# Converting weights beside pairs two and three: loads a whole tile ahead, three pieces per tile, 16 and 24 tiles

## The chip, the core and the metric

The kernel runs on one core of a Trainium2 chip. The metric is the time of one execution on the device in microseconds (us), lower is better; times of several executions are given as their median. The engines are PE (TensorE, matrix products), DVE (VectorE), ACT (ScalarE), POOL (GpSimd) and SP (SyncE, which here only issues DMAs).

## What is computed

The reference chains three parts, all on float inputs:

```python
attn = softmax(scale * q_c @ k_c.T)      # chunks of 64 rows, 8 batches x 8 heads x 576 rows
x = (attn @ v_c)                         # reshaped to 4608 x 512
x = ((x @ w_a) * (x @ w_b)) @ w_out      # first gated product, d_ff = 1536
h = ((x @ w1) * (x @ w2)) @ w3           # second gated product, d_ff = 1024
out = h @ w_out2
```

The weights of the first product are `w_a`, `w_b`, `w_out`; those of the second are `w1`, `w2`, `w3` and its own `w_out`.

## The kernel before

**Tiles and pairs.** The 4608 rows are nine blocks of 512. Eight of them go as four pairs, numbered by `sb` from 0 to 3; the last block stands alone. The program runs the first gated product over all pairs and the lone block, then the second one over them again. "Pair one, two, three" below are `sb` = 1, 2, 3 of the first product; pair zero is done by a plain scheme at the start, the others with seven products of half-size blocks (Strassen's scheme) instead of eight.

**A step.** `strassen_step` (line 873) does one block of 128 columns of the hidden width. There are 12 such steps in a pair. A step emits seven products `P5, P1, P2, P6, P3, P7, P4`, each of six matmuls (line 807), ACT copies three of them out of PSUM (line 892), DVE adds three (lines 895) and multiplies the last (line 922). PSUM banks are used again within the step, so a product waits for the eviction of an earlier one. Between them stand four parts of the output product of the step before (`Second.part`, line 836, three matmuls each). 42 + 12 = 54 matmuls of 512 columns make a step.

**Work beside the steps.** Seven times in a step `point` is called. It lets a `Track` (line 51) emit further pieces of work: each piece has a cost in estimated microseconds, and a point emits pieces until the cost done has reached its share of the total. In a pair these pieces are the attention of the next pair (`attention_pieces`, line 990: eight units beside pair two, four beside pair three) and, beside pairs two and three alone, the conversion of later weights (`later_conv`, line 1102). `merged` (line 1111) interleaves the two lists by the middle of each piece's cost. Since every engine runs its instructions in the order of emission, the place of a piece fixes what stands behind it on DVE, ACT, POOL and SP.

**The conversion.** 40 tiles of the second product's weights are converted beside pairs two and three. The weights lie in memory as 64-bit numbers, and `Conv` (line 160) makes 32-bit ones of a tile of 128 x 512. `load` (line 167, DMA on SP's queue, line 173) brings 512 KB into one of three buffers (`slot(3)`). `s1` (line 177) is one DVE operation (L179) and one of ACT (L180); `s2` (line 182) is three of DVE (L185, L188, L189) and an addition on POOL (L195). The result is stored with a DMA on ACT's queue (L157), which is put off: `store` (line 135) with wait 5 is issued after five ticks, one tick per product or part, or at the next `tick(True)`.

**The pump.** `Pump` (line 197) holds the tiles in order. `run` (line 219) issues the stores that wait, then calls `begin(self.done + 2)`, which runs `s1` of the next tile if it is loaded, then `s2` of the current one. In `later_conv` a tile has two pieces, `run` with cost 2.2 and `load` with cost 0.6. `load` asks for the tile after the next, so the load of tile i + 2 is emitted after run of tile i, and its `s1` in run of tile i + 1. The buffer of tile i + 2 is that of tile i - 1, so SP's load waits until the store of tile i - 1 has landed. Fourteen tiles stand beside pair two, the other 26 beside pair three (line 1325).

**SP's queue.** SP issues, in order of emission, the weight parts of the step after the next (`load_part`, line 710, L713 and L715, each waiting until PE has freed its buffer), the output weights (L701), the attention's loads (L148) and the conversion's loads (L173).

Of the kernel before, what the change touches and what calls it, by code (L numbers as in the profile page):

```python
# [78 lines left out]
def chunk_attention_two_gated_products(  # L79
# [30 lines left out]
    NF = [FA // P, FB // P]  # L110
# [40 lines left out]
    def tick(every=False, loads=0):  # L151
        settle(asks["done"] + loads)
        for s in stores:
            s[0] += 1
        while stores and (every or stores[0][0] > 1):
            _, to, src = stores.popleft()
            nc.scalar.dma_start(to, src)  # L157


    class Conv:  # L160
# [3 lines left out]
        def __init__(self, src, name, k=1):  # L164
            self.src, self.k, self.nm = src, k, name
# [31 lines left out]
    class Pump:  # L197
# [3 lines left out]

        def __init__(self):
            self.jobs, self.done, self.begun, self.loaded = [], 0, 0, 0
            self.cap, self.last = 0, None

        def add(self, jobs):
            self.jobs.extend(jobs)
# [11 lines left out]
        def run(self):  # L219
            assert self.done < self.loaded  # L220
            tick(True)
            last, self.last = self.last, None
            if last:
                last[0]()
            self.begin(self.done + 2)
            c, sink, eng = self.jobs[self.done]
            c.s2(eng)
            if last:
                last[1]()
            self.last = sink(c.w)  # L230
            self.done += 1
# [371 lines left out]
    def lone_pieces(x32, nm):  # L603

        xq = [pool.tile([P, 2, 2, NT], F32R, tag=f"xo{5 + K}", name=f"xl{K}{nm}") for K in range(2)]

        def one(kt):
            to = xq[kt // 2][:, kt % 2]
            split(to[:, 0], to[:, 1], x32[kt], nc.vector)

        return xq, [(0.7, False, lambda kt=kt: one(kt)) for kt in range(KM)]
# [98 lines left out]
    def load_part(ph, f, i):  # L710
        t = w_tile(4 * (f % 2) + i, f"w{ph}_{f}_{i}")
        if i < 3:
            nc.sync.dma_start(whole(t).bitcast(F32), dw[ph][f][0 if i == 0 else i + 1])  # L713
        else:
            nc.sync.dma_start(  # L715
                t[:, 0].rearrange("p s k n -> p (s k n)").bitcast(F32), dw[ph][f][1][:, NT:]
            )
        pairs.setdefault((ph, f), {})[i] = t
# [287 lines left out]
    def attention_begins(units):  # L1006
        for u in units[:2]:
            u.load1()
            u.load2()
# [11 lines left out]
    def o2_pieces():  # L1021
        got = deque()

        def load(i):
            if i < NF[1]:
                got.append(load_small(do2[i], f"o2_{i}"))

        def one(i):
            if i % 2 == 0:
                tag = ["Y0", "Y1", "Y2", "xo0"][i // 2]  # L1030
                wo2.append(pool.tile([P, 2, 2, DM], F32R, tag=tag, name=f"wo2_{i // 2}"))
            t = wo2[i // 2][:, i % 2]
            split(t[:, 0], t[:, 1], got.popleft(), nc.vector)
            load(i + 3)

        for i in range(3):
            load(i)
        return [(0.7, False, lambda i=i: one(i)) for i in range(NF[1])]

    def load_w3(n):  # L1040
        if n < 2 * NF[1]:
            w3f.append(load_small(dw3[n // 2][n % 2], f"w3_{n}"))
# [28 lines left out]
    with tc.manual_schedule():  # L1071
# [3 lines left out]
        pump = Pump()  # L1075
# [13 lines left out]
        def slot(kind):  # L1089
            slots["n"] += 1  # L1090
            n = slots["n"]
            return dict(tag=["Y0", "Y1", "Y2", "xo4", "xo5", "xo6"][n % kind])

        def conv_piece():
            def emit():
                pump.run()
                while pump.loaded < min(pump.cap, pump.done + 3):
                    pump.load(slot(6))

            return (2.9, False, emit)  # L1100

        def later_conv(n):


            def load():
                if pump.loaded < pump.done + 2:
                    pump.load(slot(3))

            return [p for _ in range(n) for p in ((2.2, False, pump.run), (0.6, False, load))]

        def merged(*lists):

# [8 lines left out]
        def unit_list(sb):  # L1121
            js = [LONE] if sb == NSB else [2 * sb, 2 * sb + 1]
            cls = TurnedOnPE if sb == 1 else Unit
            return [cls(j, hp, T) for T, j in enumerate(js) for hp in range(NHP)]
# [48 lines left out]
        for n, (T, f) in enumerate(order):  # L1173
            if T == 0:
                conv = Track([conv_piece()] * (1 if f == 0 else 3), 5 if f + 1 < AHEAD else 8)
                if f + 1 == NF[0]:
                    conv = None
# [5 lines left out]
            def point(pe=True):  # L1183
                if conv:
                    conv.point(pe)
                (at or late).point(pe)
# [18 lines left out]
        def summed(ph, f, n):  # L1205
            tag = dict(tag=f"Y{n % 3}")
            return Sums(ph, f, tag)
# [87 lines left out]
        for ph, sb in [(0, sb) for sb in range(1, NSB + 1)] + [(1, sb) for sb in range(NSB + 1)]:  # L1295
            lone = ph == 0 and sb == NSB
            begins = ph == 1 and sb == 0
            if begins:
                state["outs"] = Outs(1, 2 * NSB + 1)
            state["outs"].ahead(2)  # L1300
            if lone:
                x, pieces = lone_pieces(x32, f"{ph}{sb}")
                pieces = pieces + o2_pieces()
            elif not begins:
                x, pieces = strassen_pieces(x32, f"{ph}{sb}", sb == NSB)
            if ph == 0 and sb == 1:
                for f in range(2):
                    first_sums[f] = summed(ph, f, f)
                    first_sums[f].load()
                for f in range(2):  # L1310
                    for i in (0, 3):
                        load_part(ph, f, i)
                pieces = pieces + first_sums[0].pieces()
            steps, at, conv = NF[ph], [], []
            if ph == 0 and not lone:
                units = unit_list(sb + 1)
                attention_begins(units)
                work = attention_pieces(units)
                n_pts = PTS * steps + steps - 4
                if sb == 2:  # L1320
                    pump.cap = len(pump.jobs)
                    pump.load(slot(3))
                    pump.load(slot(3))
                if sb >= 2:
                    conv = later_conv(14 if sb == 2 else pump.cap - 14 - 3 * NF[0])
                    work = merged(work, conv)
                    n_pts = PTS * steps
                at.append(Track(work, n_pts - 3))
            if not begins:
                burst(ph, j + 1, places, pieces, [] if conv else at, state.pop("ready", None))  # L1330
            if lone:
                got = []
                for n_ in range(4):
                    load_w3(n_)
                at.append(Track(between(got), 5 * steps - 15))
                xs = {}

                def next_x():
                    diffs = deque()
                    for i in range(2):  # L1340
                        t = pool.tile([P, 4, NT], F32, tag=f"G{i}", name=f"xd{i}")
                        diffs.extend(t[:, n_] for n_ in range(4))
                    xs["x"], xs["pieces"] = strassen_pieces(got, "10", diffs=diffs)

                early = [(0.1, False, lambda: (at[0].finish(), next_x()))]
                early += [(0.7, False, lambda n_=n_: xs["pieces"][n_][2]()) for n_ in range(18)]
                late = Track(early, 11)
                class After:
                    n = 0

                    def point(self, pe=True):
                        self.n += 1
                        if self.n > 5 * steps - 15:
                            late.point(pe)

                    def finish(self):
                        late.finish()

                at.append(After())
                lone_steps(ph, x, at)  # L1360
                for p in xs["pieces"][18:]:
                    p[2]()
                x32, x = got, xs["x"]
                continue
            if ph == 1 and sb < NSB:
                got = []
                js = [LONE] if sb == NSB - 1 else [2 * sb + 2, 2 * sb + 3]
                at.append(Track(x2_pieces(js, got), PTS * steps - 3))
            j, places = block_steps(ph, sb, x, at)
            if ph == 0:  # L1370
                x32 = [u.x32 for u in units]
            elif sb < NSB:
                x32 = got
# [47 lines left out]
```

## Time and profile before

| what | value |
|---|---|
| median of 3 runs | 1804.84 us (1803.17 to 1807.74) |
| the profiled execution's own time | 1824.92 us |
| its span, first to last instruction | 1823.1 us |
| mean granted clock of TensorE | 0.948 of 2.4 GHz |
| busy: PE, DVE, ACT, POOL | 1625.3, 888.3, 552.9, 449.7 us |
| moved by DMA | 409.55 MB, mean 225 GB/s |

The profiled execution is a single one and took 20.1 us more than the median. Times inside it are told from the start of its span. Busy time of an engine is the time in which it executes, waits not counted. The granted clock is the share of full speed that the chip's throttle gave to TensorE, at one of two levels at any moment, 1.2 or 2.4 GHz. L12 is line 12 of the kernel; SPq and DVEq are an engine's queue. "A <- B" in a wait means that A waited for B; in an instruction "out<-in" are the tiles that it writes and reads. The tiles of the conversion are `cv_o`, `cv_w` and `cv`, by the weight that they come from.

### The profile page before, as it was taken

Reading aid. Unit: us, or ns where it says so; the run is one execution under the profiler, and the core shown is the slowest. Engines: PE = TensorE matmul, PEld = TensorE weight load, DVE = VectorE, ACT = ScalarE, POOL = GpSimd, SP = SyncE. Lnnn points to the kernel's source line nnn. Section 1 sums busy time; section 2 is a strip of 40 time slices with the busy share of each in tenths; the row PEclk is TensorE's granted clock in tenths of the full one; section 3 lists DMA queues with packets and bytes.
Section 4 is the critical chain, followed back from the end, with each engine's and each line's share of the span. In section 5 each row is a group of like instructions: output and inputs, shape, how many; then the busy total and the mean of one; then the engine's idle time right before and its main releaser. Section 6 shows DMA issues by size and latency. Waiting matters only on the chain.

```text
span 1823.1 us, 24483 instructions
## 1 busy us (share of the span) xinstructions
PE 1625.3 (89%) x8968; PEld 1289.9 (71%) x8968; DVE 888.3 (49%) x1460; ACT 552.9 (30%) x989; POOL 449.7 (25%) x350
## 2 busy tenths in 40 slices
PE   5789999889998887897887797999999999999998
PEld 3567777667776665675665676778877877878887
DVE  5658756565763554564455533345234252252231
ACT  4434434222242221242221242223132142242232
POOL 1223323111141221242232240001232231231232
PEclk8789999999999998998898898999999999999999
DMA  8658766776778677586775577878666666676685
GB/s 209 219 172 262 254 202 173 226 215 188 246 223 238 194 199 205 193 249 221 231 228 191 194 256 265 325 296 300 208 225 225 208 222 228 208 231 208 196 280 176
DMA packets 302071, 409.55 MB, mean 225 GB/s; under 512 B 176000, under 2 KB 196480, under 8 KB 301952
## 3 DMA queue, kind: packets, MB, share of 16 engines
q1 hardware_dynamic: 265568, 318.85, 57.9%
q10 hardware_dynamic: 36384, 89.14, 12.8%
q8 instruction: 71, 1.16, 0.3%
q14 instruction: 48, 0.39, 0.1%
HBM read 321.91 MB, written 85.98 MB: 224 GB/s over the span
## 4 chain that ended last, share of the span: by engine, by line
PE 40%; DMA 5%; DVE 2%; issue 2%; POOL 1%; ACT 1%; SPq 0%; ACTq 0%; POOLq 0%; DVEq 0%
PE P L807 22%; PE acc L836 12%; PE wf L1060 3%; DMA cv<-in_moe_w_dram 2%; PE pa0L L793 2%; PE pb0L L793 2%; DMA d<-cv 1%; DMA wo<-dwo 1%; DMA w<-dw 0%; DVE c L895 0%; PE w3p L1050 0%; ACT ev L845 0%; DMA su<-d 0%; DMA x2d<-ev 0%; POOL gl_5b L243 0%
## 5 line engine op out<-in xcount | busy, mean ns | idle before, releaser
L807 PE MATMUL P<-xP,w 128*128 128x512 f32 (+1 forms) x3192 | 777.0, 397 | 102.1 <-DVE c L895 51.2
L807 PEld LDWEIGHTS P<-xP,w 128*128 128x128 f32 x3192 | 597.2, 196 | 249.9 <-DVE c L895 60.8
L895 DVE TENSOR_TENSOR c<-P,c 128x512 f32<-128x512 f32 (+1 forms) x228 | 149.7, 660 | 341.4 <-PE P L807 332.6
L892 ACT COPY c<-P 128x512 f32<-128x512 f32 (+1 forms) x228 | 128.1, 564 | 229.2 <-PE P L807 219.8
L923 POOL TENSOR_TENSOR G<-c,c 128x512 f32<-128x512 f32 x68 | 88.5, 1302 | 416.5 <-DVE c L895 416.2
L242 ACT CAST gh<-c 128x512 fp32r<-128x512 f32 x68 | 42.2, 621 | 356.0 <-DVE c L922 342.1
L836 PE MATMUL acc<-gh,wo 128*128 128x512 f32 x384 | 145.1, 415 | 0.0
L243 POOL TENSOR_TENSOR gl<-c,gh 128x512 fp32r<-128x512 f32 x68 | 90.0, 1324 | 172.7 <-ACT gh L242 172.7
L836 PE MATMUL acc<-wo,gh 128*128 128x512 f32 x320 | 111.3, 391 | 0.5 <-ACT gh L242 0.5
L922 DVE TENSOR_TENSOR c<-P,c 128x512 f32<-128x512 f32 x68 | 46.9, 690 | 129.2 <-PE P L807 129.2
L836 PEld LDWEIGHTS acc<-gh,wo 128*128 128x128 f32 x384 | 76.5, 199 | 17.9
L195 POOL TENSOR_TENSOR cv<-cv 128x512 f32<-128x512 f32 x40 | 46.2, 1155 | 149.6 <-DVE cv L189 118.1
L793 PE MATMUL pa<-xq,w 128*128 128x512 f32 x288 | 78.0, 422 | 1.0 <-ACT xq L242 0.8
L836 PE MATMUL acc<-gl,wo 128*128 128x512 f32 x192 | 78.6, 409 | 0.0
L793 PE MATMUL pb<-xq,w 128*128 128x512 f32 x288 | 72.0, 400 | 0.8 <-DVE G0p L946 0.8
L845 ACT COPY ev<-acc 128x512 f32<-128x512 f32 x72 | 42.3, 588 | 95.2 <-PE acc L836 85.5
L836 PEld LDWEIGHTS acc<-wo,gh 128*128 128x128 f32 x320 | 60.1, 188 | 14.0 <-ACT gh L242 1.0
L793 PEld LDWEIGHTS pa<-xq,w 128*128 128x128 f32 x288 | 57.3, 204 | 14.9 <-ACT xq L242 1.6
L243 DVE TENSOR_TENSOR xP<-xP,xP 128x512 fp32r<-128x512 f32 (+1 forms) x56 | 46.7, 875 | 35.4 <-ACT xP L242 35.4
L836 PE MATMUL acc<-wo,gl 128*128 128x512 f32 x160 | 63.1, 394 | 0.8 <-POOL gl L243 0.8
L793 PEld LDWEIGHTS pb<-xq,w 128*128 128x128 f32 x288 | 54.5, 192 | 12.7 <-DVE G0p L946 1.2
L243 DVE TENSOR_TENSOR xP<-x,xP 128x512 fp32r<-128x512 f32 (+1 forms) x48 | 55.9, 1209 | 2.0 <-ACT xP L242 2.0
(149 smaller groups left out, 2291.8 us busy)
## 6 DMA issues: line engine op xcount, KB each, us to landing
w<-dw SPq DMA_DIRECT2D x228, 512.0 KB, 4.4
wo<-dwo SPq DMA_DIRECT2D x168, 512.0 KB, 4.6
dw<-w ACTq DMA_DIRECT2D x48, 512.0 KB, 5.2
w<-dw SPq DMA_DIRECT2D x92, 256.0 KB, 3.2
d<-cv ACTq DMA_DIRECT2D x40, 256.0 KB, 4.3
su<-d SPq DMA_DIRECT2D x20, 512.0 KB, 5.6
cv_o<-in_moe_w_out_dram SPq DMA_DIRECT2D x18, 512.0 KB, 5.3
x2d<-ev ACTq DMA_DIRECT2D x36, 256.0 KB, 4.7
```

The costliest lines, as they stand in the source:

```text
L195: eng.tensor_tensor(self.w, hi.bitcast(F32), lo, op=ALU.add)
L242: nc.scalar.copy(dst_h, src)
L243: eng_l.tensor_tensor(dst_l, src, dst_h, op=ALU.subtract)
L793: nc.tensor.matmul(ps, w[m][:, kk // 2, wp, kk % 2], xq[kk // 2][:, kk % 2, xp], start=(n == 0), stop=(n == 3 * KM - 1),)
L807: nc.tensor.matmul(ps, w[:, wp, kt], x[:, kt, xp], start=(begins and n == 0), stop=(n == 5), skip_group_check=True,)
L836: nc.tensor.matmul(acc[m], a, b, start=(f == 0 and (wp, gp) == SEQ[0]), stop=(f == NF[ph] - 1 and (wp, gp) == SEQ[-1]),)
L845: nc.scalar.copy(t, acc[m])
L892: nc.scalar.copy(t, src)
L895: add = lambda o, a, b: nc.vector.tensor_tensor(o, a, b, op=ALU.add)
L922: nc.vector.tensor_tensor(g, last, c11, op=ALU.mult)
L923: nc.gpsimd.tensor_tensor(g_place(ph, nm.split("_")[0], f, gplaces), c22, c12, op=ALU.mult)
L1060: nc.tensor.matmul(ps, t[:, gp, jj], wo2[jj // 2][:, jj % 2, wp], start=(jj == 0 and (wp, gp) == SEQ[0]), stop=(jj == NF[1] - 1 and (wp, g ...
```

## The change

`Pump` gets a field `ahead`, 2 at first, which `run` adds to the number of tiles done in place of the constant 2. `later_conv` sets it to 1, so that from pair two on `run` begins no tile beyond its own. A piece of its own, with cost 0.5, begins the next tile; `run` has cost 1.8 in place of 2.2 and the load 0.3 in place of 0.6. The load of tile i + 2 is still emitted after run of tile i, but its `s1` now comes after run of tile i + 1. Sixteen tiles stand beside pair two instead of 14, and 24 beside pair three instead of 26.

```diff
         def __init__(self):
             self.jobs, self.done, self.begun, self.loaded = [], 0, 0, 0
-            self.cap, self.last = 0, None
+            self.cap, self.ahead, self.last = 0, 2, None
...
             if last:
                 last[0]()
-            self.begin(self.done + 2)
+            self.begin(self.done + self.ahead)
             c, sink, eng = self.jobs[self.done]
...
         def later_conv(n):
 
+            pump.ahead = 1
 
             def load():
                 if pump.loaded < pump.done + 2:
                     pump.load(slot(3))
 
-            return [p for _ in range(n) for p in ((2.2, False, pump.run), (0.6, False, load))]
+            begin = lambda: pump.begin(pump.done + 1)
+            one = [(0.5, False, begin), (1.8, False, pump.run), (0.3, False, load)]
+            return one * n
...
                 if sb >= 2:
-                    conv = later_conv(14 if sb == 2 else pump.cap - 14 - 3 * NF[0])
+                    conv = later_conv(16 if sb == 2 else pump.cap - 16 - 3 * NF[0])
```

## Rows read from the trace of the kernel before

**Rows 1.** The page's chain that ended last, shares of the span by line.

```profile
PE P L807 22%; PE acc L836 12%; PE wf L1060 3%; DMA cv<-in_moe_w_dram 2%; PE pa0L L793 2%; PE pb0L L793 2%; DMA d<-cv 1%; DMA wo<-dwo 1%; DMA w<-dw 0%; DVE c L895 0%; PE w3p L1050 0%; ACT ev L845 0%; DMA su<-d 0%; DMA x2d<-ev 0%; POOL gl_5b L243 0%
```

**Rows 2.** The chain of waits over 900 to 1070 us, shares by line.

```profile
by line: PE P L807 31.3%; DMA cv<-in_moe_w_dram 23.3%; PE acc L836 13.6%; DMA d<-cv 6.7%; issue 3.1%; DVE cv L179 2.6%; DMA dw<-cv_w 2.6%; DVE cv L185 2.2%; DMA w<-dw 2.2%; DVE cv L189 2.1%; DVE c L895 1.9%; DVE cv L188 1.5%; ACT ev L845 1.
```

**Rows 3.** Stages: us; busy PE, PEld, DVE, ACT, POOL; clock; DMA share; GB/s.

```profile
330.00:517.00 187.00, 169.91 (x1123) 131.85 (x1123) 114.32 (x216) 51.31 (x97) 31.40 (x24) 0.96 0.74 221
562.00:778.00 216.00, 178.05 (x1139) 136.76 (x1138) 116.96 (x220) 47.29 (x88) 46.05 (x38) 0.90 0.70 209
828.00:1050.00 222.00, 171.56 (x854) 130.69 (x855) 114.44 (x203) 46.59 (x81) 56.88 (x49) 0.85 0.68 213
1254.00:1353.00 99.00, 99.00 (x431) 80.57 (x430) 24.07 (x35) 22.20 (x38) 21.02 (x17) 1.00 0.71 234
```

**Rows 4.** Waits of PE, 562 to 778: total us, times, longest us.

```profile
PE P L807 <- DVE c L895: 15.6, 5, 5.8
PE P L807 <- ACT c L892: 14.7, 5, 4.0
```

**Rows 5.** Waits of PE, 828 to 1050.

```profile
PE P L807 <- DVE c L895: 26.5, 6, 7.7
PE P L807 <- ACT c L892: 13.2, 6, 5.4
PE P L807 <- DVE c L922: 10.6, 3, 6.0
```

**Rows 6.** Waits of DVE, 562 to 778.

```profile
DVE cv_w L179 <- DMA cv_w<-in_moe_w_dram: 23.0, 5, 10.8
DVE cv_o L185 <- ACT cv_o L180: 15.8, 1, 15.8
DVE cv_o L179 <- DMA cv_o<-in_moe_w_out_dram: 14.0, 4, 5.4
```

**Rows 7.** Waits of DVE, 828 to 1050.

```profile
DVE cv L179 <- DMA cv<-in_moe_w_dram: 37.1, 9, 7.9
DVE cv_w L179 <- DMA cv_w<-in_moe_w_dram: 18.7, 4, 7.6
```

**Rows 8.** Chain of waits (start, us, what), then PE's timeline with idle before.

```profile
1003.01 6.54 DMA cv<-in_moe_w_dram
...
1009.62 0.43 DVE cv L179
...
1014.41 2.93 PE L807 MATMUL P<-xP,w 128*128 128x512 f32 x6 [5.36 <-DVE c L895]
```

**Rows 9.** The conversion's operations: ns min/median/max, first and last start.

```profile
L179 DVE TENSOR_SCALAR cv<-cv x40: 414/424/1512, 14.6 to 1030.8; 128x512 int32<-128x512 int32 x40
L180 ACT ACTIVATE cv<-cv x40: 657/682/703, 16.6 to 1031.3; 128x512 f32<-128x512 f32 x40
L185 DVE SCALAR_TENSOR_TENSOR cv<-cv x40: 679/685/993, 17.3 to 1037.7; 128x512 int32<-128x512 int32 x40
L188 DVE TENSOR_SCALAR cv<-cv x40: 426/428/1539, 18.0 to 1038.8; 128x512 int32<-128x512 int32 x40
L189 DVE SCALAR_TENSOR_TENSOR cv<-cv x40: 692/694/1720, 18.5 to 1040.2; 128x512 f32<-128x512 uint32 x40
```

**Rows 10.** DMA issues, 828 to 1050: count, KB each, median us to landing.

```profile
cv<-in_moe_w_dram SPq DMA_DIRECT2D x16, 512.0 KB, 5.4
```

**Rows 11.** Pair one, 330 to 517, the products: busy, mean | idle before.

```profile
L807 PE MATMUL P<-xP,w 128*128 128x512 f32 x504 | 129.1, 407 | 15.0 <-DVE c L895 6.3 <-DVE c L922 3.7 <-ACT c L892 3.1
```

**Rows 12.** SP's queue, 828 to 1050: waits for stores of converted tiles.

```profile
SPq L173 <- DMA dw<-cv_w: 14.1, 5, 6.5
```

**Rows 13.** Chain of waits: a unit's scores on PE.

```profile
946.54 0.62 PE s L345 x32
```

**Rows 14.** Six microseconds of pair three, columns as in rows 3.

```profile
856.00:862.00 6.00, 3.59 (x11) 2.56 (x11) 3.51 (x7) 1.45 (x3) 1.26 (x2) 0.78 0.98 373
```

## The prediction

> **What bounds the kernel now.** I read the page first, then the chain of waits, then the stages one by one. The chain that sets the end is almost all TensorE, yet one DMA stands in it ahead of every other transfer: the load of a weight tile to be converted [rows 1]. Cut to pair three, that load holds 23% of the chain beside 31% for the products [rows 2]. So one stage, not the whole kernel, is held by it. Next I read the stages [rows 3]: the twelve Strassen steps of pair one (330 to 517 us, no conversion), of pair two (562 to 778), of pair three (828 to 1050), and eight clean steps of the second product. The clean steps keep PE busy all of the time at full clock, 99.0/8 = 12.4 us a step. Pair two takes 216 us with PE idle for 216 - 178 = 38, pair three 222 us with 222 - 171.6 = 50.4 idle; their granted clocks are 0.90 and 0.85, which is time at 1.2 GHz instead of 2.4.
>
> Who ends PE's idle time is named as DVE or ACT evictions [rows 4, 5], but these are not slow; they come late. DVE itself stands at L179, the first operation of a tile's conversion, until the load lands: 14.0 + 23.0 us in pair two [rows 6] and 37.1 + 18.7 in pair three [rows 7], with further waits there put down to other releasers. One instance in full: the load is issued at 1003.01 and takes 6.5 us, L179 starts only then, the conversion and two additions follow, and PE resumes at 1014.41 after standing since 1009.05 [rows 8]. Its next six matmuls take 2.93 us; at full clock six take 12.4/54 x 6 = 1.4.
>
> **Why the load is late.** The order of emission, counted by hand from costs and merge: before, the piece that loads tile i+2 stands after run(i), and the first operation of tile i+2 is emitted inside run(i+1). Between them lie 1 to 3 of a step's seven points in pair two (mean 2.0) and 0 to 2 in pair three (mean 1.1). A point lasts 216/84 = 2.6 us, so the lead is about 5.1 and 2.9 us, and the load takes 5.4 us at the median [rows 10]. It must be late.
>
> **The change, part by part.**
>
> *Later first operation.* With ahead = 1 and a piece of its own, the first operation of tile i+2 moves behind run(i+1). The same count gives a lead of 5 to 7 points in pair two (mean 6) and 3 to 5 in pair three (mean 4). With the stage times below a point lasts 2.1 us, so the leads are 12.7 and 8.2 us against 5.4. Most of the 38 and 50.4 us of idle PE, and the low clock that follows them, should go.
>
> *What stays.* Floors first. Clean steps are 12 x 12.4 = 148.8 us. Attention adds scores and sums, 0.62 us each per unit [rows 13]: 8 units 9.9 us, 4 units 5.0. Floors: 158.7 and 153.8 us. PE's busy time above them, 178.1 - 158.7 = 19.4 and 171.6 - 153.8 = 17.8 us, is what the low clock costs. Late next are DVE's ordinary bunches of work. Pair one shows them without any conversion load: 15.0 us idle before products in 187 us, clock 0.96 [rows 3, 11]. DVE was 61% busy there; it would be 68% in pair two (117.0 plus 4.5 for two more tiles, over 178) and 64% in pair three (114.4 - 4.5, over 173). I charge each pair 12 us of idle PE, between nothing (clean steps) and the 15 of pair one, nearer to that one, plus 7 us of low clock (0.04 x 187 = 7.5 in pair one). That gives 158.7 + 19 = 178 and 153.8 + 19 = 173: gains of 38 and 49, together **87 us**.
>
> *Three pieces instead of two.* The conversion's instructions are the same: DVE 0.42, 0.69, 0.43, 0.69, ACT 0.68 [rows 9]. They come in smaller bunches, which can only shorten a wait behind them. New is that in ten of pair three's 24 tiles, by the same count, the first operation and the run fall on one point, so L185 waits for ACT's rescaling at L180, which used to be a whole tile earlier. Bounds: 0.7 us each if ACT is free, or 15.8 as in the one such wait of before [rows 6]. I take 1 us of DVE each and nothing on PE, inside the 12 above: DVE has over 60 us free there. If that cover goes, it is 10 us.
>
> *16 and 24 tiles.* Two tiles move from pair three to two: 4.5 us of DVE, 1.4 of ACT, two POOL additions, two loads and two stores (1.6 MB), already in the busy shares above; the sum is nothing, since each stage has slack on these.
>
> *Queues.* SP's load also waits until the store from the same buffer, three tiles before, has landed: 14.1 us over five waits in pair three [rows 12]. From run to load it is now 1.9 points of 2.06 us instead of 2.1 of 2.64, so SP may stand 1.6 us longer per tile, 38 us over 24 tiles. Behind it queue weight loads, which are asked for nearly two steps before use (over 20 us), and attention loads. I charge nothing; without that cover it is the 38 us. On ACT's queue the stores stand where they stood.
>
> *Clock.* The granted clocks put 20% of pair two and 30% of pair three at the low level; rows price that at 19.4 + 17.8 = 37 us. The Trainium skill (TensorE: Matmul & The Clock Gate, HAM oscillation) counts half of the throttled time as lost, an estimate of 21.6 + 33.3 = 55 us here; by it the sum would gain up to 18 us more. The rows decide, because much of that low-clock time is idle time already counted.
>
> *A price against the change.* Conversions beside GpSimd work show a few long DVE operations, 1.51 us for 0.42 at worst [rows 9]. The Trainium skill (SBUF — State Buffer, SBUF: two separate sides) says that DVE and GpSimd exclude each other on a shared port for a whole instruction; the worst rows agree. The medians say that it is rare, and a denser stage raises it little, so the sum stays as it is.
>
> **The sum.** The profiled execution took 1824.9 us (span 1823.1): 1824.9 - 87 = 1738. It stands 20 us above the median of the runs shown, 1804.84. If that surplus is general, the median becomes 1718; if it lay in these stalls, 1738. I take a point between: **1726 us**.
>
> **Rivals.**
> 1. *Transfers set the pace.* Pair three moves 222 x 213 = 47.3 MB. If no stage can move more than the 234 GB/s of the clean steps, pair two needs (45.1 + 1.6)/0.234 = 200 us and pair three 195: the gain is 43, and the time about 1804.8 - 43 = 1762. For it: DMA engines are busy 0.70 and 0.68 of the stages already, so 151 us of work each must fit in 175. Against it: 6 us at 373 GB/s in the middle of pair three [rows 14], and the clean steps are limited by PE, not by transfers. It also covers loads that lengthen and are late again.
> 2. *The rescaling takes the place of the load (slower).* In ten tiles of pair three DVE stands at L185 for ACT, which stands in turn for a product's end. It decides from 87/10 = 8.7 us each; at the 15.8 of the one row [rows 6] it costs 158, and the time is 1805 + 71 = 1876. Against it: that row is from the stage's start, when ACT was still emptying the sums, and ACT needs only a product (1.4), an eviction and the rescaling, some 3 us.
> 3. *The load is no earlier in time.* SP reaches it only behind weight loads that wait for PE, so it lands as late as before: 1805. For it: the load at 1003.01 was itself issued behind such a wait. Against it: three to seven points are three to seven products on PE as well.
>
> **How the numbers follow.** Forecast 0.72, transfers 0.20, no earlier 0.04, slower 0.04. Low end: all idle and low-clock time of both pairs goes except a few us, a gain near 115, 1690. High end: transfers with some loss, 1770. About 0.3% (5 us) is what a measurement can tell from no change. Faster 0.93, same 0.03, slower 0.04.
>
> **What the changed profile would show.** Right: L179 waits for conversion loads fall from 93 us in all to under 20; pair two and three last about 178 and 173 us with clocks near 0.96; PE's idle time there falls from 88 to about 25; the load leaves the top of the chain. Wrong: L185 waiting for L180 in tens of us (rival 2), products waiting for weights or a DMA share near 0.9 with L179 still waiting (rival 1), or stage times unchanged (rival 3).

## The result, and the profile after

The changed kernel takes 1745.26 us in the median (1738.38 to 1748.09, 4 runs) against 1806.29 us (1803.17 to 1809.16, 4 runs): a ratio of 0.9657, 95% interval 0.9623 to 0.9691, or 61 us less. The profiled execution took 1748.09 us, 77 less than that of before.

The stages of the changed kernel, each from its first to its last product on PE; the columns are those of [rows 3], pairs one, two and three in order:

```profile
336.00:520.00 184.00, 168.45 (x1116) 130.81 (x1115) 114.48 (x215) 50.14 (x95) 31.38 (x24) 0.95 0.74 221
562.00:765.00 203.00, 173.53 (x1148) 134.37 (x1147) 124.78 (x228) 48.83 (x90) 48.62 (x40) 0.93 0.77 232
806.00:973.00 167.00, 157.49 (x891) 124.11 (x890) 116.46 (x200) 49.06 (x86) 56.97 (x48) 0.98 0.87 286
```

The same three stretches of the kernel before, bounded in the same way:

```profile
332.00:517.00 185.00, 167.91 (x1115) 130.21 (x1114) 113.61 (x214) 50.14 (x95) 31.40 (x24) 0.96 0.74 220
560.00:778.00 218.00, 180.05 (x1147) 138.40 (x1147) 116.96 (x220) 48.38 (x90) 46.05 (x38) 0.90 0.70 209
819.00:1050.00 231.00, 180.55 (x893) 137.64 (x893) 115.13 (x204) 50.22 (x88) 56.88 (x49) 0.86 0.68 214
```

Pair three gave 64 us and pair two only 15; pair one stood still. (The windows of [rows 3] were a little short: pair three's left out 9 us at its start, pair two's 2 us, and PE was busy throughout both.) PE's idle time is the stretch less its busy time: in pair two it fell from 38 to 29.5 us, in pair three from 50.5 to 9.5, with granted clocks of 0.93 and 0.98.

DVE's waits of the changed kernel say what was removed and what was not: first pair two, which answers to [rows 6], then, after the dots, pair three, for [rows 7].

```profile
DVE cv_w L179 <- DMA cv_w<-in_moe_w_dram: 21.8, 5, 8.1
DVE cv_o L185 <- ACT cv_o L180: 14.1, 1, 14.1
...
DVE kT L334 <- DMA v<-in_v_dram: 8.3, 1, 8.3
DVE kT L334 <- DMA qk<-in_k_dram: 5.7, 2, 3.5
DVE cv_o L179 <- DMA cv_o<-in_moe_w_out_dram: 2.5, 3, 1.4
...
DVE cv_w L185 <- ACT cv_w L180: 17.5, 5, 13.1
...
DVE cv L185 <- ACT cv L180: 5.6, 7, 0.9
...
DVE cv L179 <- DMA cv<-in_moe_w_dram: 4.2, 3, 1.9
```

In pair three the waits for the load at L179 have gone from 37.1 + 18.7 us to 4.6 (4.2, and one of 0.4 at cv_w). In pair two 24.3 us (21.8 + 2.5) remain of 37, and a new kind stands beside them: at L334, where the attention turns its k tile, 14.0 us for the attention's own loads. Both kinds of load stand in SP's queue.

SP's waits in pair two, the kernel before and then, after the dots, the changed one:

```profile
SPq L713 <- PE P L807: 32.9, 12, 5.6
SPq L715 <- PE P L807: 20.2, 7, 6.0
...
SPq L713 <- PE P L807: 17.1, 9, 7.6
SPq L148 <- DMA dw<-cv_w: 13.5, 3, 5.2
SPq L148 <- DMA do<-cv_o: 11.5, 6, 3.8
SPq L148 <- DMA cv_w<-in_moe_w_dram: 6.7, 4, 3.0
```

A queue that waits for PE is ahead of it. Before, SP waited 53 us for PE to free weight buffers (L713, L715); now 17 at L713 and 3 at L715, and more for other DMAs. SP has fallen behind, and so the lead in its program is no lead in time. The attention's loads (L148) are seen to wait for stores of converted tiles, with which they share no data: in the trace every DMA of SP and ACT signals one of eight semaphores, taken in turn, and waits until the DMA before it on that semaphore has landed. (In the changed kernel's trace there are 1140 pairs of successive DMAs on one of the eight with a known landing; in none was the second issued before the first had landed.) SP's waits that a DMA ended grew from 34 to 54 us in pair two.

### The profile page after: what moved, and what is told of

It is laid out like the page before. It is cut to its first block, busy times and chain, and to the rows that moved or that the text cites. A ratio compares the mean times of both kernels' runs of the same rounds, so it can differ in the third digit from the quotient of the medians.

```text
span 1746.3 us, 24482 instructions
## 1 busy us (share of the span) xinstructions
PE 1595.2 (91%) x8968; PEld 1272.0 (73%) x8968; DVE 896.6 (51%) x1460; ACT 552.6 (32%) x989; POOL 452.1 (26%) x350
## 4 chain that ended last, share of the span: by engine, by line
PE 67%; DMA 11%; DVE 10%; SPq 4%; issue 3%; ACT 3%; POOL 1%; ACTq 0%; POOLq 0%; DVEq 0%
PE P L807 33%; PE acc L836 18%; PE pa L793 3%; PE pb L793 3%; SPq L148 3%; PE wf L1060 3%; DMA wo<-dwo 2%; PE pa0L L793 2%; PE pb0L L793 2%; DVE c L895 1%; PE x L396 1%; DMA su<-d 1%; DMA qk<-in_k_dram 1%; DMA cv_w<-in_moe_w_dram 1%; DMA v<-in_v_dram 1%
## 5 line engine op out<-in xcount | busy, mean ns | idle before, releaser
L807 PE MATMUL P<-xP,w 128*128 128x512 f32 (+1 forms) x3192 | 750.4, 388 | 44.0 <-DVE c L895 27.1
L807 PEld LDWEIGHTS P<-xP,w 128*128 128x128 f32 x3192 | 582.4, 191 | 180.6 <-DVE c L895 35.9
L836 PEld LDWEIGHTS acc<-gh,wo 128*128 128x128 f32 x384 | 75.4, 196 | 17.5
L793 PEld LDWEIGHTS pa<-xq,w 128*128 128x128 f32 x288 | 57.0, 203 | 14.8 <-ACT xq L242 1.4
L243 POOL TENSOR_TENSOR gl0L<-sa0L,gh0L 128x512 fp32r<-128x512 f32 x12 | 16.0, 1333 | 159.8 <-ACT gh0L L242 159.8
```

What stands on the lines that cost most here:

```text
L243: eng_l.tensor_tensor(dst_l, src, dst_h, op=ALU.subtract)
L793: nc.tensor.matmul(ps, w[m][:, kk // 2, wp, kk % 2], xq[kk // 2][:, kk % 2, xp], start=(n == 0), stop=(n == 3 * KM - 1),)
L807: nc.tensor.matmul(ps, w[:, wp, kt], x[:, kt, xp], start=(begins and n == 0), stop=(n == 5), skip_group_check=True,)
L836: nc.tensor.matmul(acc[m], a, b, start=(f == 0 and (wp, gp) == SEQ[0]), stop=(f == NF[ph] - 1 and (wp, gp) == SEQ[-1]),)
```

## The experiments

All were profiled and timed in three rounds beside the kernel before. Their times are compared as ratios to it, since they ran on three different chips: it took 1811.67 us in the first four runs, 1808.38 in the next three and 1808.84 in the last three.

**Counts alone.** The kernel before with 16 and 24 tiles:

```diff
-                    conv = later_conv(14 if sb == 2 else pump.cap - 14 - 3 * NF[0])
+                    conv = later_conv(16 if sb == 2 else pump.cap - 16 - 3 * NF[0])
```

> The kernel before with only the tile counts changed to 16 and 24; load, first operation and run stand as before. Theory (the lead paid): 1795 to 1812, L179's waits for conversion loads stay near 90 us in all. Rival (the counts paid): 1785 or less.

Measured: 1809.38 us, ratio 0.9996 (0.9972 to 1.002). DVE's waits for the loads over both pairs stay where they were:

```profile
DVE cv_w L179 <- DMA cv_w<-in_moe_w_dram: 56.2, 11, 9.1
DVE cv_o L179 <- DMA cv_o<-in_moe_w_out_dram: 22.1, 6, 6.8
DVE cv L179 <- DMA cv<-in_moe_w_dram: 21.4, 10, 4.3
```

The sum of these is 99.7 us against 92.8 before. Pairs two and three of this run:

```profile
556.00:776.00 220.00, 175.20 (x1148) 134.29 (x1147) 123.70 (x228) 49.53 (x92) 47.32 (x40) 0.91 0.73 215
817.00:1030.00 213.00, 172.56 (x892) 132.64 (x891) 111.54 (x197) 48.54 (x85) 55.11 (x47) 0.90 0.72 224
```

By the medians the counts alone do nothing. The profiles, single executions, show pair three 18 us shorter than in the kernel before (231) and pair two 2 longer, but that kernel's profile lies some 20 us above its median and this one (1804.12 us) 5 below. So part of the 64 us of pair three may be that surplus. Against this trace, which has the same counts, the change gives 17 us in pair two and 46 in pair three, 63 together, near the 61 of the medians.

**Pieces alone.** The changed kernel with the counts of before, the same line the other way round:

```diff
-                    conv = later_conv(16 if sb == 2 else pump.cap - 16 - 3 * NF[0])
+                    conv = later_conv(14 if sb == 2 else pump.cap - 14 - 3 * NF[0])
```

> The changed kernel with the tile counts of before, 14 beside pair two and 26 beside pair three. Theory (the lead of the load is what paid): the time stays within 8 us of the changed kernel's 1745, pair two a few us shorter than its 201, pair three a few us longer than its 169; waits of L179 for conversion loads stay near 30 us. Rival (the counts paid, because pair three had too many tiles): at least 20 us of the 61 are lost, 1765 or more, and pair three lasts over 185.

Measured: 1751.85 us, ratio 0.9681 (0.9654 to 0.9707), beside 0.9657 of the change. Nearly all of the gain is the pieces'. Pairs two and three:

```profile
561.00:758.00 197.00, 171.15 (x1148) 132.90 (x1147) 117.70 (x220) 48.18 (x89) 46.55 (x38) 0.92 0.78 231
799.00:981.00 182.00, 163.42 (x893) 126.59 (x892) 123.84 (x210) 50.48 (x89) 59.59 (x50) 0.95 0.84 271
```

In these single executions the two tiles are worth 15 us to pair three and cost pair two 6; between the kernels' ratios the intervals overlap.

**Split without lead.** Three pieces and the new counts, but the first operation runs a tile ahead of the run, as before:

```diff
-            pump.ahead = 1
+            pump.ahead = 2
-            begin = lambda: pump.begin(pump.done + 1)
+            begin = lambda: pump.begin(pump.done + 2)
```

> The changed kernel with ahead = 2 kept: three pieces of cost 0.5, 1.8 and 0.3 and counts 16 and 24, but the piece that begins works on the tile after the next run's, as before, so the load has a lead of 0.9 points in pair two and 0.5 in pair three, less than the 2.0 and 1.1 of the kernel before; L179 and L185 of a tile lie a whole tile apart. Theory (the lead pays; the split pays only because it parts L179 from L185): 1800 to 1840, not faster than the kernel before, L179's waits for loads 90 us or more. Rival (three small pieces pay by themselves): 1785 or less.

Measured: 1834.16 us, ratio 1.0142 (1.0107 to 1.0177): 1.4% slower than the kernel before. With its lead cut by half, the load is later still: DVE's waits at L179 over both pairs come to 139 us against 118 before. Of these 86 us are put down to the conversion's own loads, where 90 or more were expected.

**Lead without split.** The first operation inside its own tile's run:

```diff
-            begin = lambda: pump.begin(pump.done + 1)
-            one = [(0.5, False, begin), (1.8, False, pump.run), (0.3, False, load)]
+            one = [(2.3, False, pump.run), (0.3, False, load)]
```

> The changed kernel with the tile's first operation back inside run, but inside the run of its own tile: two pieces of cost 2.3 and 0.3, counts 16 and 24. The load is now about 1.5 tiles ahead, and L185 follows L179 on DVE at once, so that it waits for ACT's L180 in every tile. Theory (the lead paid, the split did little): 1740 to 1765; L185's waits for L180 rise to 30 to 60 us in all, since each costs some 0.8 us on DVE. Rival (the smaller bunches on DVE paid): 1780 or more.

Measured: 1771.22 us, ratio 0.9787 (0.9761 to 0.9813), so faster than the kernel before by 2.1%, and 6 us over the upper end of what the theory expected. DVE's waits over both pairs:

```profile
DVE cv_w L185 <- ACT cv_w L180: 35.5, 16, 15.8
DVE kT L334 <- DMA qk<-in_k_dram: 31.2, 5, 7.9
DVE cv_o L185 <- ACT cv_o L180: 21.1, 8, 14.2
DVE cv L185 <- ACT cv L180: 16.0, 16, 2.1
```

The load is on time here (L179's waits for it come to 10 us), yet 24 us of the gain are missing. L185 now waits for ACT's L180 in every one of 40 tiles, 73 us in all against 37 in the changed kernel; without the one long wait at the start of each pair it is 43 against 10. Its waits at L334 grew too, to 31 us from 14. So the lead is the first part of the gain. The split adds to it, most visibly by leaving ACT time between L179 and L185; how much of the 24 us is this and how much the later k loads was not parted. The run before gives no sign that smaller pieces pay by themselves, though its lead is shorter as well.

**Conversion loads on POOL's queue.**

```diff
-                    pump.load(slot(3))
+                    pump.load(slot(3), nc.gpsimd)
```

> The changed kernel with the conversion's loads beside pairs two and three issued from POOL's queue instead of SP's. Theory for what is left in pair two (SP's queue, full of the attention's small loads, runs behind and brings the conversion's loads late): L179's waits in pair two fall from 24 us to under 8, pair two lasts 190 or less instead of 201, the time is 1725 to 1738. Rival (the transfers themselves are slow, DMA share 0.77 in pair two): loads land as late as before, pair two stays within 5 us of 201. Second rival: POOL stands for a buffer's store and brings its own products late, slower than 1750.

Measured: 1750.45 us, ratio 0.9687 (0.9651 to 0.9722). The theory's first number came out, its second and its time did not: in pair two L179 waits for no load any more, but the pair still lasts 197 us. Its row, then DVE's longest wait there, which is another:

```profile
556.00:753.00 197.00, 171.10 (x1149) 133.00 (x1148) 124.80 (x228) 49.50 (x91) 57.62 (x56) 0.95 0.80 240
...
DVE kT L334 <- DMA qk<-in_k_dram: 26.1, 5, 7.4
```

The attention's loads are late instead. And in pair three, which SP held up little, POOL now waits at L173 for the stores that free the buffers (12.4 + 4.4 + 2.6 us), and the pair lasts 180 us instead of 167. So it is not the conversion's loads that must leave SP in pair two.

**One DMA for each attention tile.** The units beside pair two bring each q, k and v tile with a single DMA; bytes and piece size are the same, the rows are not, so the attention of the last pair is computed from wrong rows:

```diff
+                if self.j in (6, 7):
+                    rows = src.rearrange("b h s (e d) -> (b h s e) d", d=32)
+                    r0 = 2048 * (4 * (self.j - 6) + self.hp)
+                    ask(tv, rows[r0 : r0 + 2048, :].rearrange("(t p) d -> p t d", p=P))
+                    continue
...
```

> The changed kernel, but beside pair two each q, k and v tile of the attention comes with one DMA instead of about six: as many bytes, in the same pieces of 128 and 256 bytes, from other rows, so the attention of the last pair is computed from the wrong rows; every other instruction is the same. Theory (in pair two SP's queue is behind, because 151 small attention loads stand in it and only eight DMAs are under way at a time): DVE's waits at L179 and at L333 and L334 fall from 38 us to under 10, pair two lasts 175 to 185 instead of 203, the time is 16 to 28 us below the changed kernel. Rival (the bytes and small packets themselves are slow, DMA share 0.77): those waits stay over 25 us, pair two stays over 195. Pair one, which is left alone, stays at 184 in both.

Measured: 1718.5 us, ratio 0.9509 (0.947 to 0.9548). Pair two, then SP's two longest waits in it:

```profile
569.00:737.00 168.00, 162.45 (x1148) 128.07 (x1147) 124.79 (x228) 49.41 (x91) 49.26 (x40) 0.99 0.89 275
...
SPq L726 <- PE P L820: 59.1, 29, 4.1
SPq L728 <- PE P L820: 29.3, 10, 4.3
```

Pair two falls from 203 to 168 us, below the theory's range, with PE idle for 5.5. DVE waits for no load in it. Pair one, left alone, took 189 us, somewhat more than its 184. SP (L726 and L728 are L713 and L715 here) waits 88 us for PE and so is ahead again. As many bytes in as small pieces pass at 275 GB/s. So the size of the pieces did not make the loads late; what changed is how many DMAs SP issues, 91 in the pair instead of 227. That the other rows themselves made no difference was not tested.

**Eight tiles beside pair two, 32 beside pair three.**

```diff
-                    conv = later_conv(16 if sb == 2 else pump.cap - 16 - 3 * NF[0])
+                    conv = later_conv(8 if sb == 2 else pump.cap - 8 - 3 * NF[0])
```

> The changed kernel with 8 tiles beside pair two and 32 beside pair three. Theory (SP's queue is behind in pair two because of the attention's loads, not the conversion's): pair two keeps DVE waits at L333 and L334 of 20 us or more, as pair one has them without any conversion, and lasts 185 to 193. Pair three has a buffer's round of store and load to fit into a shorter time per tile: 185 to 205 us, so the whole is slower than the changed kernel by 5 to 25 us. Rival (the conversion's loads hold pair two): pair two falls to 175.

Measured: 1764.22 us, ratio 0.9752 (0.9715 to 0.979). Pair two lasts 190 us with half of the tiles and 17.5 us of waits at L333 and L334, though none at L179; pair three lasts 200 us. The waits are a little under the 20 us expected; the rest is as the theory had it: pair two does not fall to 175, and its late loads are the attention's.

**The attention's v loads on POOL's queue**, beside pair two alone (as shown), then beside pairs one to three (`self.j >= 4` instead), then k as well:

```diff
-            nc.sync.dma_start(*asks["left"].popleft())
+            to, src, queue = asks["left"].popleft()
+            (queue or nc.sync).dma_start(to, src)
...
+        def vq(self):
+            return nc.gpsimd if self.j in (6, 7) else nc.sync
```

> The changed kernel with the v loads of the attention beside pair two, 55 of its 151 small loads, issued from POOL's queue. Theory (SP's queue): SP issues 30 us less there, waits at L179, L333 and L334 fall from 38 us to 15 to 25, pair two lasts 188 to 197, the time is 5 to 15 us below the changed kernel. Rival (POOL stands for a free v buffer and its products come late): no gain or slower.

> The changed kernel with the attention's v loads beside pairs one, two and three issued from POOL's queue. Theory (SP's queue): as with pair two alone for that pair, 183 to 190, and pair one gains 5 to 12 of its 184; 1716 to 1726. Rival (pair one is held by something else): 1728 to 1732.

> The changed kernel with the attention's k and v loads beside pairs one, two and three issued from POOL's queue, q from SP's. Theory (SP's queue): pair two loses most of what is left, idle PE falls from 17.6 us with v alone to under 10, pair two lasts 172 to 182; pair one, which has the same waits at L333 and L334 without any conversion, falls from 184 to 175 or less; 1705 to 1722 in all. Rival (POOL, with 100 issues of 0.55 us each in a pair beside its 48 us of work, brings gl and the sums late): no better than v alone, 1728 or more.

Measured: v beside pair two 1727.99 us, ratio 0.9547 (0.9497 to 0.9598); v beside all three 1719.95 us, ratio 0.9511 (0.9478 to 0.9543), the fastest version with the whole computation; k and v 1758.31 us, ratio 0.9722 (0.9682 to 0.9761). The first gained more than the 5 to 15 us expected, 20 by its ratio. Its pair two, and then the three pairs with v on POOL throughout:

```profile
560.00:746.00 186.00, 168.39 (x1148) 131.70 (x1147) 125.07 (x229) 49.03 (x90) 78.13 (x92) 0.96 0.81 248
...
336.00:505.00 169.00, 161.80 (x1116) 126.32 (x1115) 114.75 (x214) 49.62 (x94) 65.18 (x84) 1.00 0.77 234
547.00:735.00 188.00, 169.13 (x1148) 132.21 (x1147) 124.56 (x229) 49.19 (x90) 78.25 (x92) 0.95 0.81 246
778.00:949.00 171.00, 158.92 (x891) 125.49 (x890) 120.46 (x201) 49.13 (x86) 64.14 (x60) 0.97 0.85 278
```

Pair one, which has no conversions, gains 15 us as well, from 184 to 169, and runs at full clock. Pair two gains 15, from 203 to 188. With k on POOL too, pair one is still shorter than in the changed kernel (175 us) and pair two as short as with v alone, but PE then stands between pairs two and three. Its longest wait from 748 to 810 us, and POOL's groups there:

```profile
PE acc L842 <- POOL gl_5b L244: 19.2, 3, 11.4
...
L244 POOL TENSOR_TENSOR gl_5b<-G,gh_5b 128x512 fp32r<-128x512 f32 x11 | 14.4, 1327 | 0.1
L149 POOL DMA_DIRECT2D v<-in_v_dram x12 | 7.1, 598 | 1.8 <-issue 1.8
L149 POOL DMA_DIRECT2D qk<-in_k_dram x8 | 5.3, 668 | 19.9 <-issue 19.9
```

POOL stands 19.9 us before k loads (the profile shows nothing that it waits for), and the operands of the output product behind them come late. A queue that may wait is best put on an engine for which nobody waits just then; this rival held for k, not for v.

## Why the prediction came out as it did

**The cause was right.** The load at L179 held pair three and part of pair two; a longer lead removed it. Lead alone and split alone show it from both sides, and the counts do nothing by themselves. Of the signs named, L179's waits for loads fell from 93 us to 29, where under 20 was named, and idle PE from 88 to 39, where 25 was; both miss in pair two.

**Pair three: right, its size a little low.** Forecast 173 us, measured 167: idle PE 9.5 us where 12 were charged, and PE's busy time 157.5 - 153.8 = 3.7 us over the floor where 7 were charged. As the stage was 9 us longer before than the window read, its gain is 64 us, not 49. The short windows hid busy time, and so the low clock was priced too small as well: over the whole stretches PE's busy time above the floors was 180.0 - 158.7 = 21.3 and 180.5 - 153.8 = 26.7 us, 48 in all and not 37.

**Pair two: the step that failed.** Forecast 178 us, measured 203: idle 29.5 us where 12 were charged, and 173.5 - 158.7 = 14.8 us of low clock where 7 were. The step is the one on queues, "I charge nothing", together with the one on what stays, which named DVE's ordinary bunches of work as late next. Late next were the attention's loads, and with them what is left of the conversion's. SP issues some 150 of them in pair two; with them it falls behind PE, and a lead of six points in the program is too little on the clock: DVE still stood for the load in 8 of 16 tiles (24.3 us). One DMA per tile in their place gave pair two 168 us, less even than forecast. The price of 38 us that was kept as the other end came from the wait for a store at L173, and that wait was not what mattered. In pair two SP has none of it in the changed kernel; in pair three it grew, from 19.7 us to 31.4, and the loads were on time all the same:

```profile
SPq L173 <- DMA d<-cv: 22.1, 9, 5.4
...
SPq L173 <- DMA dw<-cv_w: 9.3, 2, 8.1
```

The sign was in the profile of before. Pair one, taken as the measure of what stays [rows 11], had the same trouble. Its waits of DVE in the kernel before were

```profile
DVE kT L334 <- DMA qk<-in_k_dram: 10.1, 4, 6.5
DVE kT L334 <- DMA v<-in_v_dram: 5.7, 1, 5.7
```

and the idle time was read there as DVE's own work. With v on another queue pair one's idle PE falls from 15.6 us in the changed kernel to 7.2.

**The rescaling on one point: right.** Charged 1 us each in ten tiles; pair three shows eleven short waits at L185, of 0.7 to 1.7 us and 10.0 us in all, and one of 13.1 that, like the 14.1 of pair two, belongs to the stage's start. Rival 2 did not come.

**The transfers: not the pace.** Pair three moved 286 GB/s, well over the 234 of rival 1, and pair two 275 with one DMA per tile.

**From the profile to the median.** The stages gave 15 + 64 = 79 us, where 87 were forecast. That the sum came so near is in part luck: pair two gave 23 us less than forecast and pair three 15 more, and the two misses met. The profiled execution fell by 77 and the median by 61, because the surplus of 19 us over the median of four runs shrank to 3. Of the two readings, the one that put the surplus into the stalls (1738) was the better one; the point between them (1726) lay 19 us low, 8 of them from the sum and the rest from this.

**Still open.** What of SP's lag is the issuing itself (114 us of 203 in pair two) and what is the waiting for one of eight semaphores (54 us) was not parted. With v on POOL beside pair two SP's issuing falls to 78 us and its waits that a DMA ended do not fall (65 us), yet the pair is 17 us shorter; with one DMA per tile the issuing is 62 us and those waits are gone, and it is 35 us shorter. So fewer issues pay without shorter waits; what the waits cost by themselves is not shown. In pair two with v on POOL, 12.9 us of waits at the turning of k remain, and no changed version here removes them with the whole computation.

## What to carry to other kernels

A load is ahead only if its queue is ahead: before counting on a lead in the program, see in the queue's waits whether it waits for the consumer (then it is ahead) or the consumer for it. Once one late transfer is removed, the next is likely to be its neighbour in the same in-order queue, and the number of DMAs there can matter more than their bytes. When one tile's work goes from an engine to another and back, a gap between its two halves on the first engine spares it a wait for the second.

## What the runs showed of the hardware and was not expected

In this program the DMAs of SP and ACT together use eight completion semaphores in turn, and those of POOL eight others. A load on SP can thus wait for a store that ACT has not issued yet: in the changed kernel's pair two SP stands before a k load from 684.65 to 689.88 us, for a store that ACT issues only at 685.94. Issuing a small v load keeps POOL busy for 0.58 us (52 of them beside pair two), about as long as SP (0.62). Moving some 55 of some 150 small loads to POOL shortened pair two by 17 us. The Trainium skill (DMA: Bandwidth & Descriptors, Issuing engines are not separate DMA queues) says that DMAs run on the same DMA engines whichever engine starts them, and that starting them on several saves no more than the time of issue, which is usually small beside the DMA itself. One issue is small here too (0.62 us against some 4 us from issue to landing), but for a queue that is behind the sum of them was not: SP's issuing in the pair fell by 36 us, from 114 to 78, and the kernel became faster, from a ratio of 0.9657 to 0.9547.
